# Transposes as two 64-row halves, the middle column once a batch, and a narrowing with fewer VectorE steps, in a fused Performer attention and FNet kernel

## The chip, the cores and the metric

The kernel runs on one core of one Trainium2 chip. The metric is the device time of one execution in microseconds. The times and the profile are taken on the chip. A profile comes from one execution, and its time is not exactly the median of the timed runs. The engines are called PE (TensorE products), PEld (TensorE weight loads), DVE (VectorE), ACT (ScalarE), POOL (GpSimd) and SP (SyncE, which issues the DMAs).

## The reference

Everything is float32 at the end; the inputs come as float64 and are narrowed on the chip. B = 8 batches, H = 8 heads, S = 576, D = 64, 128 random features, model width 512, hidden width 2048.

```python
# attention with positive random features
q_p, k_p = phi(q * scale), phi(k * scale)   # phi(x) = exp(h - max(h)), h = x @ omega.T - |x|^2/2
kv, z = k_p.T @ v, k_p.sum(over s)
x = (q_p @ kv) / (q_p @ z + 1e-6)           # heads side by side: (B, 576, 512)
# Fourier mix and MLP
u = x + real(fft(fft(x, axis=1), axis=2))
un = (u - mean(u)) / sqrt(var(u) + 1e-6)
out = u + relu(un @ w_ch1) @ w_ch2
```

## The kernel before

The program has two stages. The first works through attention, the Fourier mix, the loading and narrowing of the weights, four plain blocks of 128 tokens of the MLP and the sums of weights that the second stage needs. The second stage does the other 4096 tokens, in eight blocks of 512, with a Strassen-like scheme of seven products: `first_of` (L1310) makes the hidden layer, and `product_of` (L1490) the output.

The order of all instructions is written out ahead. Each piece of work is a generator that yields a `Step` (engine or engines, a planned duration, the events it needs, the buffers and PSUM banks it takes and gives) and then issues its instructions. `Listing.run` picks the next step. In the first stage the string `PICKS` says which, one character for a step: the place of the stream in the list of waiting ones, and whether a step that two engines can do goes to the second. In the second stage the planner itself picks by planned times. Every engine, and SP's DMA queue, then runs its own list in this order. An instruction that waits holds up all that is behind it on its engine.

PSUM has eight banks. `take=("bank",)` takes one and `take=("duo",)` takes two adjoining ones that begin at an even number. A bank is given back by the step that empties it.

**Attention** (`attn`, 32 head pairs, three streams of them at a time). The rows of k and q of a pair are nine and nine in a tile `kq`. `transposed` turns nine 128x128 squares of it (L512) into banks in groups of 4, 4 and 1, each group into one bank, and `evicted` copies a group to `kqT` on ACT (L528) or DVE (L526). `pairs_of` multiplies by omega (L606): the first six pairs with tiles of 64 rows and all 128 columns of the array ("wide"), the others with tiles of 64 by 64. `softmax` takes row maxima (L549, DVE) and exponentials (L566, ACT) into `e`. Products with v follow (L640, 64 by 64 tiles). Then nine squares of the queries' features are turned in groups of 1, 4 and 4 (L512 again, to `qeT`), multiplied (L687, L695, tiles of 128 by 64) and divided into x (L716 on DVE, or ten scaled copies L712 on ACT).

**Mix** (`mix`, once a batch). `folds` adds and subtracts mirrored rows and columns (L743 to L779, DVE or POOL). The transform along the tokens is L799 and L809, copied to `y` by ACT (L822). Then for each of three blocks of rows c (128, 128 and 64 rows) L849 does the transform along the width. The middle column of the fold goes a way of its own: after L849 in each block, four products of one column each (L860, two records each) put its transform into one more column of the same bank. `residual` fetches the bank with ACT (L893), the column with it, and combines and adds to x (L898 to L911).

**Narrowing** (`narrow`, 32 slabs of 128x512, two 32-bit words a number, `lo` and `hi`). The high word is scaled by ACT (L439) or POOL (L437); DVE takes the sign (L442), shifts and joins (L444), takes the exponent (L447) and scales the low word with it (L449). POOL or DVE adds the two (L455). A weight so made is what L1099 and L1122 of the plain blocks and the sums of weights wait for.

**Norms and plain blocks.** `norm_of` normalises 128 tokens; for the plain blocks and for the first large one it turns four squares on PE into one bank (L1035), which ACT copies out (L1039). `plain_of` has the products L1099 (hidden) and L1122 (output). They fill PE between attention steps.

**Sums of w2** (`w2_parts`). For each of seven factors, up to eight subtractions (L1196, POOL or DVE) make summed quarters of w2, and five stores (L1219, L1221) send them to `w2l` in memory. The next factor's subtractions wait for all five.

Of the kernel before, what the change touches and what calls it, by code (L numbers as in the profile page):

```python
# [39 lines left out]
class Clock(NamedTuple):  # L40
# [16 lines left out]
DIGITS = "0123456789abcdefghijklmnopqrstuvwxyzABCDEFGHIJKLMNOPQRSTUVWXYZ!#$%&()*+,"  # L57
# [6 lines left out]
    "40e0f03eafdaegebg3NbcbeefdcOdeccfgdb37ghj0gjj7hlP79Kj7ik97i8S7efhjffeHldfPiehdjfdOShgihidaKOdbRhciff"  # L64
    "ecgOfeejdfdPdeeedgSfdffdOfd8Kiii88jhd8jP8b99i8e8jcddghjgheiifcecdciieicgPgdef9cdghbkededfgchbggb79ij"
    "8hi7hjaPN97aj9gfffeg8eif8hcej1jccc7ehidbhffLiQObfbeG766gggfcbjahj9Ofghhjj8dgkkgT6jghff8de6dUjfhbgegh"
    "MefRafjUf8jgciSjeckkhjakkaeikggjlioklnRSgodonON7l7l6nnj9icadc97cibPJIej788a7edhclhkmjjagVijihkkfpVim"
    "oklilTTillaghlhnmVjkmpjkhhnmkimlgglmbjpjjg9d9alafhhdjlacdTback0j766k7lh4g89Gck6gkki77gij5ijhgj6dimni"
    "3ndjgi6Kc4jldlaikbkaijbhf75dcjlmUVUDGci45jciekajkkUk5kihoUeaeobaiodlenMSdonbiiljjcWjjkboijjkkhgMfkik"
    "hiflkmOFF99nol5m8jT7naabda89Rbj97ecdl8cjilegiPkQb4acahg57ebbgabgdjkdTkk6eceebb5f9dg4RGce486ggg6egfhh"  # L70
    "fg4g9egf5cbdRgfhhhcgjhggejigibbmHnbedijj6Neb7biihi9bgihckaffPa8cijdhbdghbaeibdefffacjiciQSfi9JJ75ih5"
    "jgjI699ajfg6g7fgefd65bO6Kalkkgd5jgjikagfldliPJpeoaeeOPQNejadgilgicljiSSFe65k56kl5Hk7j67S9lilk9gliih6"
    "ffUgec4fg4dbgg7fedaif5gfbheefilddddddeQhg9kbfncggRcfkkafkag6ngb65p5Hopoj4bhoaXbelli68bjjl5b7dlhiQRhi"
    "lflhpkgiWomjknmmmUimnjbjhnJjkm5akPFgedccff6Wf7idUVhi8Th3fogbqp8fgmkeidjna7ckeXYghmnmffnjeo79q6547oa4"
    "nlkpd7aceonnc8bViVicilbhmjim8fh7Snn8l5mkkPjgfRhfhihg8ghfbS4kjf83j4lllb79jei8mnUblfnmmiolpilOki9Mh5l5"
    "pmnaOm79jjVmkbblekFiji9a9kffjgjikhiihfgjafhgfigh4g50fff0ba5fdh9dghda77hgfdcbg8eO988jcehefibjjkellPcc"
    "fcdhgcihPgcffba2f82b3c98cbcdcd6a299efgddb9KGQQbefLa9ecf74gg9867RgP9idg8kgOhePP7be6ff2e5cc8fbMgdaf8f8"
    "9hd9bM999bddc7cdb7ec9effegd7ibhgeQ8hKf7ccghRlUikh7m5lWmm5dkMQ6M71fS6d1gdb99747ifddh8fdhhdhfdbihgiljn"
    "gWgijgQ93ekal8kEhIIbT3jjagkb9k9eTfhkhlje34m49974i666h68fa7e6eHK79982975a894a39M8cM8b4aK7ab984fgO8ebc"
    "J8b86ce8Pb5fc9cbe6caff3a9b94f8dIQe9abd876e9fdcFPdb7ffbf99SS8RiLa4a7gPbajfgg8gdfhg2i2787Hf6OcdIN5d3LH"  # L80
    "accd46ddeaa72d9c7bbaa4bb9a9bc7c0777dghhdP7Bfddebd76ff1fddIe9949438686bcGaca8F348dHc67a5be95Hb55d15E4"
    "9Gc1F5a9a6844634458E584E59189970955888574443113301110"
# [39 lines left out]
class Listing:  # L122
# [4 lines left out]
    def __init__(self, buffers):  # L127
        self.clock = FIRST
        self.free = dict.fromkeys((PE, ACT, DVE, POOL, SP, NONE, PORT), 0.0) | self.clock.begin
        self.buffers = {name: [0.0] * n for name, n in buffers.items()}  # L130
        self.made = {}
        self.moved = 0.0
        self.mode = "whole"
        self.banks = [0.0] * 8
        self.got = None

    def banks_at(self, n, t):
# [3 lines left out]
        for i in range(0, 8, n):  # L141
# [6 lines left out]
    def start(self, step, ready, before, other=False):  # L148
# [30 lines left out]
        engines = sorted(step.engines, key=lambda e: begin(e) + step.engines[e])  # L179
        eng = engines[other and len(engines) > 1]  # L180
# [3 lines left out]
    def run(self, streams, picks=None):  # L184
        todo = []
        picks = iter(picks or ())
        clock = self.clock
# [15 lines left out]
        while todo:  # L203
            pick = next(picks, None)
            other, n = divmod(DIGITS.index(pick), 36) if pick else (0, 0)
# [75 lines left out]
def kernel(  # L281
# [128 lines left out]

    tabs = _tables(S, DM)
# [15 lines left out]
    def narrow(i, dst, raw):  # L427
# [3 lines left out]
        lof, hif, bits = lo.bitcast(F32), hi.bitcast(F32), dst.bitcast(U32)  # L431


        step = Step({ACT: 0.57, POOL: 1.48}, after=(("raw", i),), port=True, bias=1.11)
# [3 lines left out]
        else:  # L438
# [4 lines left out]
        yield Step(DVE, 1.05, port=True, bias=0.36)  # L443
# [3 lines left out]
        nc.vector.tensor_scalar(sign[:], bits, 0xFF800000, None, op0=ALU.bitwise_and)  # L447
        yield Step(DVE, 0.61, give=("sign",), port=True, bias=-0.99)
        nc.vector.scalar_tensor_tensor(  # L449
            lof, lo, 2.0**-52, sign[:].bitcast(F32), op0=ALU.mult, op1=ALU.mult  # L450
        )
        step = Step({POOL: 1.25, DVE: 0.61}, makes=("w", i), give=("slab",), port=True, bias=1.25)
        yield step
        eng = nc.gpsimd if step.eng == POOL else nc.vector
        eng.tensor_tensor(out=dst, in0=dst, in1=lof, op=ALU.add)  # L455
# [38 lines left out]

    def transposed(src, name, groups, after, makes, give, order=None):
# [3 lines left out]
        for j0, j1 in groups:  # L499
# [3 lines left out]
                0.109 * m,  # L503
                after=after(j0, j1),
                take=("bank",) + (("turned",) if j0 == 0 else ()),
# [5 lines left out]
            for j in range(j0, j1):  # L511
                nc.tensor.transpose(ps[:, (j - j0) * 128 : (j - j0 + 1) * 128], src(j), ident[:])  # L512
            yield Fork(evicted(dst, b, j0, j1, makes, order))
        return dst

    def evicted(dst, b, j0, j1, makes, order):
# [13 lines left out]
        ps = psum_of(b)[:, 0 : 128 * (j1 - j0)].rearrange("q (c p) -> q c p", p=128)  # L530
        dst = dst[:, j0:j1, :]
        if order is None:
            copy(dst, ps)
            return
        h, s, t = order[j0]
        dst = dst.rearrange("q c p -> q (c p)").rearrange("q (h s t c) -> q s h t c", h=h, s=s, t=t)
        ps = ps.rearrange("q c (h t s) -> q s h t c", h=h, s=s)
# [35 lines left out]
    def attn(n):  # L573
# [9 lines left out]
            ((0, 4), (4, 8), (8, R)),  # L583
# [8 lines left out]
        def pairs_of(js, *ts):  # L592
# [3 lines left out]
                (0.25 if wide else 0.23) * len(js),  # L596
                mode="rows" if wide else "quarters",
                after=(("kqT", n, js[-1] // 4 * 4), "om2"),
# [24 lines left out]
        def feature(c):  # L623
# [6 lines left out]
            1.1,  # L630
# [18 lines left out]
        def keep():  # L649
# [23 lines left out]
            1.22,  # L673
# [54 lines left out]
    def mix(b):  # L728
# [5 lines left out]
        mid_t = small.tile([P, NC3, 1], F32, name="mid", tag="mid", bufs=2)  # L734

        def folds(n):
            op = (ALU.add, ALU.subtract)[n]
            even, odd = (ALU.subtract, ALU.add) if n else (ALU.add, ALU.subtract)
            step = Step({DVE: 1.135, POOL: 2.75}, take=("half",), port=True)
# [15 lines left out]
            step = Step({DVE: 0.91, POOL: 1.55}, port=True)  # L755
            yield step
            eng = nc.gpsimd if step.eng == POOL else nc.vector
            for dst, o in ((NC3, ALU.add), (1, ALU.subtract)):
# [7 lines left out]
                {DVE: 1.2, POOL: 2.2},  # L766
# [11 lines left out]
            middle = fold[:, :, 3, 0:1] if n else mid_t[:]  # L778
            eng.tensor_copy(out=middle, in_=h[:, 1 : NC3 + 1, QD : QD + 1])  # L779

        yield from folds(0)
        yield Fork(folds(1))

# [47 lines left out]
        for c in range(NC3):  # L831
# [3 lines left out]
                1.38 if c < NL else 0.94,  # L835
                mode="whole" if c < NL else "halves",
                after=tuple(("y", b, n) for n in range(2)) + ("cd", "sd"),
# [17 lines left out]
            def middle(i):  # L855

                g, odd = divmod(i, 2)
                rows = slice(64 * odd, 64 * odd + 64) if g else slice(0, 128)
                k1 = HK * odd + k0 + NK * g
                nc.tensor.matmul(  # L860
                    ab[p1 + w * odd : p1 + w * odd + w, 1, KD : KD + 1],
                    lhsT=cs[rows, k1 : k1 + w],
                    rhs=mid_t[rows, 1 if g else NL * (1 - odd), :],
                    start=g == 0,
                    stop=g == 1,
                    skip_group_check=True,
                )
# [4 lines left out]
            for i in range(4):  # L872
                middle(i)
# [758 lines left out]
```

## Time and profile before

| | us |
|---|---|
| median of three runs | 1166.79 |
| lowest and highest | 1164.52, 1167.47 |
| profiled execution: time | 1174.67 |
| profiled execution: span | 1172.2 |
| granted TensorE clock, mean | 0.996 |
| first L1310 product starts (end of the first stage) | about 424 |

| engine | busy us in the span | share |
|---|---|---|
| PE | 1153.5 | 98% |
| PEld | 1032.9 | 88% |
| DVE | 754.7 | 64% |
| ACT | 436.8 | 37% |
| POOL | 430.4 | 37% |

A busy time is the union of an engine's instructions. A PE record runs from its start until its last result is out (0.27 us for 128 columns), while the next may start 0.109 us after it, so PE's busy time does not say how full the array is; distances from start to start do. A float32 product gives two records, a transpose only one. Idle time of an engine is put down to what released the instruction after it.

### The profile page before, as it was taken

How to read it: one execution, taken by the hardware profiler on the slowest of the kernel's cores; microseconds unless marked ns; L12 is line 12 of the kernel's file. 1: busy time of each engine (PE TensorE's matmuls, PEld its weight loads, DVE VectorE, ACT ScalarE, POOL GpSimd, SP SyncE). 2: the span in 40 equal slices, each digit the busy share in tenths (PEclk: the TensorE clock that was granted, in tenths of full speed). 3: DMA queues.
4: the chain of work that ended last, by engine and by line, in shares of the span. 5: the costliest groups of instructions: out<-in, count | busy, mean ns of one | idle time of the engine just before them, and what ended most of it. 6: DMA issues, size and time to landing. Idle time of an engine off the chain costs nothing.

```text
span 1172.2 us, 31328 instructions
## 1 busy us (share of the span) xinstructions
PE 1153.5 (98%) x12437; PEld 1032.9 (88%) x12437; DVE 754.7 (64%) x1573; ACT 436.8 (37%) x1485; POOL 430.4 (37%) x496
## 2 busy tenths in 40 slices
PE   8999999999999999999999999999999999999998
PEld 7888888779777868998998998898999899899898
DVE  5999999986676655744754664573573574474255
ACT  6998898866444212122112212212212212221211
POOL 2433444455472106225225324413513512522421
PEclk8999999999999999999999999999999999999999
DMA  7866765665662254873783593694495396388055
GB/s 218 224 188 186 240 181 178 203 210 163 207 196 101 77 162 139 263 264 85 222 278 112 172 308 99 152 317 141 112 319 190 82 290 231 83 258 263 35 166 203
DMA packets 167217, 220.34 MB, mean 188 GB/s; under 512 B 50080, under 2 KB 81056, under 8 KB 167072
## 3 DMA queue, kind: packets, MB, share of 16 engines
q1 hardware_dynamic: 166576, 218.09, 60.7%
q8 instruction: 98, 1.61, 0.6%
q14 instruction: 47, 0.39, 0.1%
q10 hardware_dynamic: 496, 0.26, 0.1%
HBM read 179.24 MB, written 43.25 MB: 190 GB/s over the span
## 4 chain that ended last, share of the span: by engine, by line
PE 88%; DMA 5%; DVE 4%; ACT 2%; SPq 1%; issue 1%; DVEq 0%
PE banks L1310 33%; PE banks L1490 27%; PE banks L1099 5%; PE banks L606 5%; PE banks L1122 4%; PE banks L512 4%; DMA wl<-w2l 3%; PE banks L640 2%; PE banks L687 2%; PE banks L849 2%; PE banks L799 1%; ACT e L566 1%; DVE nmx L549 1%; DMA kq<-in_k_dram 1%; PE banks L809 1%; PE banks L860 1%
## 5 line engine op out<-in xcount | busy, mean ns | idle before, releaser
L1490 PE MATMUL banks<-wl,sums 128*128 128x128 f32 x1792 | 217.4, 275 | 0.0
L1490 PEld LDWEIGHTS banks<-wl,sums 128*128 128x128 f32 x1792 | 208.6, 192 | 0.0
L1296 DVE CUSTOM_DVE_ANT_0 hid<-banks,s 128x256 f32<-128x256 f32 x192 | 80.9, 424 | 188.8 <-PE banks L1310 188.8
L566 ACT ACTIVATE e<-banks,nmx 128x128 f32<-128x128 f32 x576 | 165.3, 434 | 23.2 <-DVE nmx L549 22.4
L1324 ACT ACTIVATE s<-banks 128x256 f32<-128x256 f32 x192 | 73.7, 384 | 259.0 <-PE banks L1310 259.0
L1310 PE MATMUL banks<-unT,w 128*128 128x256 f32 x704 | 166.3, 379 | 0.0
L1310 PEld LDWEIGHTS banks<-unT,w 128*128 128x128 f32 x704 | 133.2, 190 | 18.3 <-issue 0.5
L1530 POOL TENSOR_TENSOR ur<-ur,part 128x512 f32<-128x512 f32 x32 | 47.3, 1479 | 267.1 <-ACT part L1523 187.0
L1465 ACT ACTIVATE s<-banks 128x128 f32<-128x128 f32 x168 | 46.6, 278 | 256.7 <-PE banks L1490 220.3
L1310 PE MATMUL banks<-tt,w1s 128*128 128x256 f32 x512 | 126.3, 379 | 0.0
L1310 PEld LDWEIGHTS banks<-tt,w1s 128*128 128x128 f32 x512 | 97.0, 190 | 13.7 <-DVE hid L1296 0.4
L1490 PE MATMUL banks<-wl,hid 128*128 128x128 f32 x768 | 100.0, 276 | 3.2 <-DMA wl<-w2l 3.1
L1470 DVE TENSOR_TENSOR part<-banks,s 128x128 f32<-128x128 f32 x168 | 49.0, 292 | 83.4 <-PE banks L1490 82.2
L549 DVE TENSOR_REDUCE nmx<-banks 128x8 f32<-128x1024 f32 (+1 forms) x96 | 89.3, 951 | 19.7 <-PE banks L606 15.5
L1490 PEld LDWEIGHTS banks<-wl,hid 128*128 128x128 f32 x768 | 94.0, 192 | 6.0 <-DMA wl<-w2l 4.5
L606 PE MATMUL banks<-om,kqT 64*64 64x128 f32 (+1 forms) x2088 | 80.6, 278 | 1.9 <-ACT kv L656 1.2
L1310 PE MATMUL banks<-unT,w1s 128*128 128x256 f32 x320 | 79.5, 379 | 0.0
L606 PEld LDWEIGHTS banks<-om,kqT 64*64 64x64 f32 (+1 forms) x2088 | 65.8, 140 | 13.3 <-issue 4.3
L1490 PE MATMUL banks<-wl,hs 128*128 128x128 f32 x576 | 75.1, 275 | 0.5 <-DVE part L1470 0.4
L1490 PEld LDWEIGHTS banks<-wl,hs 128*128 128x128 f32 x576 | 70.1, 192 | 1.2 <-DVE part L1470 0.6
L1377 POOL TENSOR_TENSOR hs<-hid,hs 128x256 f32<-128x256 f32 x64 | 50.1, 784 | 57.2 <-issue 37.1
L1310 PEld LDWEIGHTS banks<-unT,w1s 128*128 128x128 f32 x320 | 60.4, 190 | 8.7
(128 smaller groups left out, 1914.6 us busy)
## 6 DMA issues: line engine op xcount, KB each, us to landing
wl<-w2l SPq DMA_DIRECT2D x392, 256.0 KB
raw<-in_moe_w_ch_dram SPq DMA_DIRECT2D x32, 512.0 KB
kq<-in_k_dram SPq DMA_DIRECT2D x32, 288.0 KB
kq<-in_q_dram SPq DMA_DIRECT2D x32, 288.0 KB
vd<-in_v_dram SPq DMA_DIRECT2D x32, 288.0 KB
u<-us SPq DMA_DIRECT2D x36, 256.0 KB
ur<-us SPq DMA_DIRECT2D x36, 256.0 KB
out_dram<-ur SPq DMA_DIRECT2D x34, 256.0 KB
```

What stands on the lines that cost most here:

```text
L512: nc.tensor.transpose(ps[:, (j - j0) * 128 : (j - j0 + 1) * 128], src(j), ident[:])
L549: nc.vector.tensor_reduce(nmx[:, :, 0:num], pps[:, :, 0 : MF * num].rearrange("p b (c m) -> p b c m", m=MF), axis=AX.X, op=ALU.max, negate ...
L566: nc.scalar.activation(out=e[:, c + (i if num == 1 else 0), :], in_=pps[:, i, MF * c : MF * c + MF], func=AF.Exp, bias=nmx[:, i, c : c + 1],)
L606: nc.tensor.matmul(pps[cols, c, MF * m : MF * m + MF], lhsT=kqT[rows, j, cols], rhs=om2[rows, :],)
L1099: nc.tensor.matmul(hp[:, 0:TP], lhsT=w1[:, dc, 128 * fc : 128 * fc + 128], rhs=unTs[key][:, dc, :], start=(dc == 0), stop=(dc == NDC - 1),)
L1296: nc.vector._custom_dve(TENSOR_ADD_SAT, out=o, in0=ps, in1=sb, s0=FMAX, s1=0.0)
L1310: nc.tensor.matmul(ps[:, 0:HT].rearrange("f (b q) -> f b q", q=Q), lhsT=left(dc), rhs=right(dc), start=start and dc == 0, stop=(dc == D2 - 1),
L1324: nc.scalar.activation(out=s[:], in_=ps[:, 0:HT], func=AF.Copy)
L1377: nc.gpsimd.tensor_tensor(out=o, in0=l, in1=r, op=op)
L1470: nc.vector.tensor_tensor(out=part[:, t, 128 * m : 128 * m + 128], in0=ps[:, 0:128], in1=saved[with_][:], op=ALU.add,)
L1490: nc.tensor.matmul(ps[:, 0:128], lhsT=left[:, f], rhs=wls[j, i, n][:, f], start=start and f == 0, stop=(f == 3), skip_group_check=True,)
L1530: eng.tensor_tensor(out=o, in0=o, in1=other, op=ALU.add)
```

## The change

- **Transposes.** `turned_by` replaces each transpose of a 128x128 square (L512, L1035) by two of 64 rows and 128 columns. The halves use rows 0 to 63 and 64 to 127 of the array and write into two adjoining banks, so a group takes a `duo`. `halves_of` is the view of the two banks that the copies read. `kqT` is turned in two groups, 4 and 5 squares, where there were three.
- **Middle column.** The four one-column products after each L849 go. A step `middles` makes those of all three blocks of a batch together, in one bank, with operands padded with zeros so that all use 128 rows, and two small ACT copies keep the result in `mid_k`.
- **Narrowing.** ACT converts the low word to an integer scaled by 2^-29, DVE's L447 and L449 go, and POOL always does the last addition, now on integers.
- **Stores of w2's sums.** One step a store in place of one for all five; the next subtractions wait for the stores of the tiles they overwrite and no others.
- **Order.** A new `PICKS`, two characters a step: stream and engine as before, and the bank. Some planned durations are changed.

```diff
 class Listing.run
-            other, n = divmod(DIGITS.index(pick), 36) if pick else (0, 0)
+            n = place(pick) if pick else 0
+            other, self.bank = divmod(place(next(picks)), 9) if pick else (None, None)
 narrow
-        lof, hif, bits = lo.bitcast(F32), hi.bitcast(F32), dst.bitcast(U32)
+        hif, bits = hi.bitcast(F32), dst.bitcast(U32)
+        def rounding():
+            yield Step(ACT, 0.57, after=(("raw", i),), makes=("low", i), bias=1.11)
+            nc.scalar.activation(out=lo, in_=lo, func=AF.Copy, scale=2.0**-29)
+        yield Fork(rounding())
...
-        nc.vector.tensor_scalar(sign[:], bits, 0xFF800000, None, op0=ALU.bitwise_and)
-        yield Step(DVE, 0.61, give=("sign",), port=True, bias=-0.99)
-        nc.vector.scalar_tensor_tensor(
-            lof, lo, 2.0**-52, sign[:].bitcast(F32), op0=ALU.mult, op1=ALU.mult
-        )
-        step = Step({POOL: 1.25, DVE: 0.61}, makes=("w", i), give=("slab",), port=True, bias=1.25)
-        yield step
-        eng = nc.gpsimd if step.eng == POOL else nc.vector
-        eng.tensor_tensor(out=dst, in0=dst, in1=lof, op=ALU.add)
+        yield Step(POOL, 1.25, after=(("low", i),), makes=("w", i), give=("slab",), port=True, bias=1.25)
+        nc.gpsimd.tensor_tensor(out=bits, in0=bits, in1=lo, op=ALU.add)
 new functions
+    def turned_by(ps, n, src):
+        y = 512 // n
+        for c in range(len(src)):
+            for a in range(2):
+                rows = slice(64 * a, 64 * a + 64)
+                out = ps[:, a].rearrange("q (h y) -> q h y", h=n)[:, :, 64 // n * c : 64 // n * (c + 1)]
+                nc.tensor.transpose(out, src[c][rows], ident[rows, rows])
+    def halves_of(ps, n, m):
+        flat = ps.rearrange("q b f -> q (b f)").rearrange("q (h y) -> q h y", h=2 * n)
+        return flat[:, :, 0 : 64 // n * m].rearrange("q h (c x) -> q h c x", c=m)
 transposed
-                0.109 * m,
+                0.03 + 0.056 * m,
+                mode="rows",
-                take=("bank",) + (("turned",) if j0 == 0 else ()),
+                take=("duo",) + (("turned",) if j0 == 0 else ()),
-            for j in range(j0, j1):
-                nc.tensor.transpose(ps[:, (j - j0) * 128 : (j - j0 + 1) * 128], src(j), ident[:])
-            yield Fork(evicted(dst, b, j0, j1, makes, order))
+            n = order[j0][0] // 2 if order else 1
+            turned_by(ps, n, [src(j) for j in range(j0, j1)])
+            yield Fork(evicted(dst, b, j0, j1, n, makes, order))
 evicted
-        ps = psum_of(b)[:, 0 : 128 * (j1 - j0)].rearrange("q (c p) -> q c p", p=128)
+        ps = halves_of(psum_of(b), n, j1 - j0)
 attn
-            ((0, 4), (4, 8), (8, R)),
+            ((0, 4), (4, R)),
 mix
-            def middle(i):
-                g, odd = divmod(i, 2)
...
-            for i in range(4):
-                middle(i)
+    def middles(b, mid_t, mid_k):
+        yield Step(PE, 0.5, mode="halves", after=(("fold", b, 0), "cs"), take=("bank",))
+        mb, ps = got()
+        for c in range(NC3):
+            w = 64 if c < NL else 32
+            for g in range(2):
+                for odd in range(2):
+                    k1 = HK * odd + 64 * c + NK * g
+                    col = 2 + odd if g else 1 - odd
+                    nc.tensor.matmul(
+                        ps[w * odd : w * odd + w, c : c + 1],
+                        lhsT=cs[:, k1 : k1 + w],
+                        rhs=mid_t[:, col : col + 1],
+                        start=g == 0, stop=g == 1, skip_group_check=True,
+                    )
+        yield Step(ACT, 0.22, give=(mb,), makes=("mid", b))
+        for c, n in ((0, P), (2, 64)):
+            nc.scalar.activation(out=mid_k[0:n, c : c + 2 - c // 2], in_=ps[0:n, c : c + 2 - c // 2], func=AF.Copy)
 norm_of
-        yield Step(PE, 0.437, take=("bank",), give=("u",))
+        yield Step(PE, 0.25, mode="rows", take=("duo",), give=("u",))
-        for dc in range(NDC):
-            nc.tensor.transpose(
-                tp[:, 128 * dc : 128 * dc + 128], u[:, 128 * dc : 128 * dc + 128], ident[:]
-            )
+        turned_by(tp, 2, [u[:, 128 * dc : 128 * dc + 128] for dc in range(NDC)])
 w2_parts
-            yield Step(SP, 3.0, 4.0, after=(("w2t", i),), kb=7 * 256, makes=("w2l", i))
             for n, t in ((0, c11), (1, c21), (4, c22)):
+                yield Step(SP, 0.6, 2.6, kb=256, makes=("w2l", i, n))
...
+            of_big = stored[0:3] if part is summed else of_big
+            of_sums = stored[3:5]
```

## The prediction

> **What bounds the kernel now.** I read the windows first, because the kernel has two stages. Up to about 424 us attention, the Fourier mix, the weight conversion and four plain blocks of the MLP share the chip. After that come the large products.
>
> ```profile
> 10.00:60.00 50.00, 47.67 (x1009) 41.10 (x1008) 44.79 (x79) 43.29 (x162) 18.10 (x12) 0.94 0.78 224
> 60.00:250.00 190.00, 187.26 (x3999) 158.64 (x3998) 178.25 (x404) 158.17 (x560) 83.72 (x86) 1.00 0.64 191
> 250.00:424.00 174.00, 171.82 (x2465) 136.39 (x2463) 114.39 (x266) 76.42 (x280) 71.22 (x73) 1.00 0.49 153
> ```
>
> Columns: stretch and length, then busy us of PE, PEld, DVE, ACT and POOL, granted clock, DMA share, GB/s. PE is busy 406.8 of 414 us. DVE comes next with 178.3 of 190 (94%) in the middle stretch, then 66%. The instruction lists of the two programs show the same PE order, instruction for instruction, from the first L1310 product on. The change therefore acts before 424 us only. The chain and PE's waits agree that PE sets this stretch:
>
> ```profile
> PE 88%; DMA 5%; DVE 4%; ACT 2%; SPq 1%; issue 1%; DVEq 0%
> PE banks L512 <- DMA kq<-in_k_dram: 2.8, 2, 2.3
> PE banks L1099 <- DVE qeT L526: 1.7, 1, 1.7
> PE banks L606 <- ACT kv L656: 1.2, 2, 0.7
> ```
>
> Waits (total us, times, longest) are small. Counting each start against the shortest start-to-start of its kind, I find 29 us lost on PE between 10 and 424 us. Hence PE time saved there should come off the end nearly one for one. Third, the groups and the order of time give the prices:
>
> ```profile
> L512 PE MATMUL banks<-ident,e 128*128 128x128 f32 x288 | 43.8, 280 | 1.8 <-DVE kqT L526 0.9 <-ACT e L566 0.9
> L512 PE MATMUL banks<-ident,kq 128*128 128x128 f32 x288 | 43.4, 287 | 2.9 <-DMA kq<-in_k_dram 2.8
> L449 DVE SCALAR_TENSOR_TENSOR raw<-raw,sign 128x512 f32<-128x512 uint32 x32 | 22.0, 687 | 0.6
> L447 DVE TENSOR_SCALAR sign<-w 128x512 uint32<-128x512 uint32 x32 | 15.2, 476 | 1.1
> L439 ACT ACTIVATE w<-raw 128x512 f32<-128x512 f32 x24 | 18.6, 788 | 3.7 <-DMA raw<-in_moe_w_ch_dram 3.7
> ```
>
> ```profile
> 30.76 1.28 PE L640 MATMUL banks<-vd,e 64*64 64x65 f32 x72
> 31.97 0.49 PE L606 MATMUL banks<-om,kqT 64*128 64x128 f32 x4
> ...
> 34.00 1.09 PE L512 MATMUL banks<-ident,e 128*128 128x128 f32 x8
> 35.02 1.16 PE L606 MATMUL banks<-om,kqT 64*128 64x128 f32 x16
> 36.11 1.09 PE L512 MATMUL banks<-ident,kq 128*128 128x128 f32 x8
> ```
>
> ```profile
> 232.83 0.60 PE L512 MATMUL banks<-ident,e 128*128 128x128 f32 x4
> ...
> 233.71 0.61 PE L849 MATMUL banks<-cd_sb,y 128*128 128x129 f32 x4
> 234.25 0.49 PE L860 MATMUL banks<-mid,cs_sb 128*64 128x1 f32 x8
> 234.67 0.71 PE L849 MATMUL banks<-sd_sb,y 128*128 128x129 f32 x4
> ...
> 236.18 0.66 PE L512 MATMUL banks<-ident,e 128*128 128x128 f32 x4
> ```
>
> Columns: start us, length, then the records; 64*128 is the part of the array used. Each run ends one pipeline latency (0.27) after its last start. So four squares in 0.60 start (0.60-0.27)/3 = 0.109 apart.
>
> **Squares as halves.** 576 squares (L512) and 32 (L1035) become 1216 half squares, whose moving side has 64 columns instead of 128. A square's 0.109 per 128 columns makes 0.055 per 64. L606's tiles of 64 rows show that two row halves run together, loads included: 16 records of 128 columns fill the 1.09 from 35.02 to 36.11, or 0.068 each, where one by one they would need 16 x 0.109 = 1.74. What could spoil it is the weight load, now as long as the product. A run behind another array shape lasts 0.66 instead of 0.60, so a square's load costs 0.06 where it is not hidden. Bounds for a pair of halves: 0.055 (load hidden) and 0.055 + 0.06 = 0.115 (not hidden: no gain). I take 0.057, because L640 is the nearest row: 18 records in each of four tiles, 65 columns and a load of their own every time, fill 31.97 - 30.76 = 1.21 less a shape change of 0.15, so 0.059. Gain: 608 x (0.109 - 0.057) = **31.6 us**; at the bounds 32.8 and -3.6.
> [...]
>
> **Shape changes.** A half square uses 64*128, so a run beside whole-array products now changes shape and one beside wide L606 no longer does. In the lists, leaving out the middle column, changes go from 193 to 236. Price: the last of eight squares starts at 34.00 + 0.06 + 7 x 0.109 = 34.82 and L606 at 35.02, 0.20 later instead of 0.109, so 0.09, and 0.06 for the exposed load: 0.15. 43 x 0.15 = **-6.5 us**.
> [...]
>
> **Middle column.** The last L849 before L860 starts at 233.71 + 3 x 0.112 = 234.05. Without L860 the next would start at 234.16; it starts at 234.67 and shows a load of 0.10 besides (0.71 against 0.61): 0.61 each time. The 64-row block costs 0.37 in the same way. Per batch 2 x 0.61 + 0.37 = 1.59, over eight 12.7 us. Now it is one run per batch of 24 records. Eight records in two shapes took 0.42, so 0.3 for the records and two or three changes of 0.15, 0.7 in all: 5.6. Gain **7.1 us** (6 to 8). Its result is fetched by two small ACT copies well before L849 asks for it.
>
> **Narrowing and the other engines.** L447, L449 and four L455 leave DVE: 15.2 + 22.0 + 2.8 = 40.0. The new assignment gives back 20 more subtractions of w2 (13.7), 34 more qeT copies (20 x 0.21 + 14 x 0.42 = 10.1) and about 10 in small pieces. DVE goes from 337 to some 331 us. ACT gains 32 conversions; no integer one is shown, and L439 (same shape and stride, 0.775 by busy time) gives 24.8. Bounds: 0.60, an L528 copy of 512 columns by busy time (29.3/49), and twice L439; I take L439. Against that it loses 30 scaled copies of x, 34 qeT copies, 25 kqT copies (a group of five in place of four and one), 13 hidden blocks and four L439, about 30 us together. POOL does all 32 final additions (4 x 1.35), now on integers: between 1.35 and 2.7 each, and I take 1.35, the row of the same shape. It loses 20 subtractions of w2 (26). So ACT stays near 276 and POOL near 160 of some 385 us, both under cover of PE; at the upper bounds ACT reaches 300 and POOL 205, still under it. If POOL's addition is late, weights arrive late, and the next to wait is L1099 behind them in PE's queue. Splitting the wait before the w2l stores lets SP issue earlier and is worth nothing on the path: SP has no share beyond 1%. The extra wait of L849 for the middle column holds up what stands behind it on PE, but its products are at least five PE runs earlier in the list.
>
> **The sum.** 31.6 - 6.5 + 7.1 = 32.2 us of PE time. PE's 29 us of loss are 7% of the stretch; with less PE work between the same DVE and ACT steps I let them grow by 3. Gain 29. The profiled execution has a span of 1172.2 and a time of 1174.7, 7.9 above the median of 1166.8. Its span would become 1143 and its time 1145.7; the median 1166.8 - 29 = **1138 us**.
>
> **Rivals.**
> *Banks (slower).* Every run of squares now takes two adjoining banks out of eight, where it took one, beside the pairs that L606, L640, L687, the mix and a bank held through L1122 need. There are 5 x 32 + 8 = 168 such runs. A mean wait of 32/168 = 0.19 us per run eats the gain; at 0.25 us the time is 1167 + 10 = 1177. For it: POOL, ACT and DVE empty these banks, and DVE stands at 94%. Against it: waits of PE for a release by ACT or DVE add up to a few us now, and a run holds its banks for half the PE time. [...]
> *Loads of the two halves do not overlap their products or each other.* Each square then costs 2 x 0.057 = 0.114: -3 - 6.5 + 7.1 makes -2.4, so 1169, no change. Against it stand L606's rows at 0.068.
> *DVE holds PE back.* If from 60 to 250 us, where DVE is 94% busy, each of the 96 reductions L549 releases PE 0.15 us later than now, 14 us go: 1152. For it, DVE sheds only 6 us in total while PE sheds 32.
> *More comes.* The first 60 us have DVE 97% busy around 20 to 50 us; the lists show 26.5 to 22.6 us of DVE work for the first four pairs, and PE's loss there could shrink. With 10 us of it gone: 1128.
>
> **How the numbers follow.** What a measurement can tell from no change is about 0.3%, 3.5 us. Forecast (1130 to 1146) 0.62, DVE 0.17, more 0.08, overlap missing 0.03, banks 0.10. Faster 0.62 + 0.17 + 0.08 = 0.87, same 0.03, slower 0.10. The range takes the first three cases, 1126 to 1158.
>
> **What would show it.** Right: stage two starts near 395 us with an unchanged length; nine squares of a pair start about 0.057 apart per square; about 250 shape changes of 0.09; L860's successor is one run of about 0.5 per batch; DVE near 86% before that point. Wrong: pairs of halves start 0.1 apart; PE's waits for ACT or DVE at the squares rise above 30 us (banks); POOL's addition well over 1.35 and L1099 waiting for it; PE busy the same but stage two no earlier.

## The result and the profile after

The kernel after takes 1184.55 us (median of four runs, 1182.08 to 1186.27) against 1167.13 us: a ratio of 1.015 [1.0125, 1.0176], 17 us slower where 29 us faster was predicted. Its profiled execution took 1184.30 us with a span of 1182.5. Stage two starts at 431.8 us and lasts 750.7, against 423.8 and 748.4 (a second profile of the kernel before gave 419.5 and 749.0). So nearly all of the loss lies before stage two. One of the four executions of g_pair_halves, an experiment below, took 1955.1 us at a mean granted clock of 0.555 and is left out of every figure. Here are the same stretches of the kernel after, and the chain of waits over the whole span:

```profile
10.00:60.00 50.00, 44.58 (x1122) 38.36 (x1120) 45.31 (x94) 45.24 (x154) 20.27 (x16) 1.00 0.72 209
60.00:250.00 190.00, 170.81 (x3685) 141.21 (x3686) 161.28 (x338) 133.93 (x438) 84.77 (x82) 0.98 0.66 203
250.00:424.00 174.00, 169.75 (x3230) 134.23 (x3229) 140.25 (x327) 98.12 (x348) 47.89 (x56) 1.00 0.45 138
```

```profile
PE 83%; DVE 7%; DMA 4%; ACT 3%; issue 2%; SPq 0%; POOL 0%; DVEq 0%; ACTq 0%; POOLq 0%
```

In the middle stretch PE falls from 187.3 to 170.8 busy us, but DVE falls as well (178.3 to 161.3) and so does ACT (158.2 to 133.9). No engine is as full as PE and DVE were (99% and 94%). The new work itself runs near its prices:

```profile
L525 PE MATMUL banks<-ident,kq 64*128 64x64 f32 x576 | 28.4, 232 | 7.0 <-DVE ht L1127 1.6 <-DMA kq<-in_q_dram 1.2 <-DVE x L754 1.0
L478 POOL TENSOR_TENSOR w<-w,raw 128x512 uint32<-128x512 uint32 x32 | 42.8, 1340 | 68.8 <-DVE w L474 29.7 <-DVE rden L742 10.8 <-ACT raw L461 8.4
L461 ACT ACTIVATE raw<-raw 128x512 uint32<-128x512 uint32 x32 | 22.7, 715 | 0.3 <-DMA raw<-in_moe_w_ch_dram 0.3
```

The order of time of PE shows both the price and what eats it:

```profile
107.86 0.77 PE L525 MATMUL banks<-ident,kq 64*128 64x64 f32 x18 [1.58 <-DVE ht L1127]
108.56 1.28 PE L678 MATMUL banks<-vd,e 64*64 64x65 f32 x72
...
132.81 1.70 PE L678 MATMUL banks<-vd,e 64*64 64x65 f32 x95
138.34 0.97 PE L678 MATMUL banks<-vd,e 64*64 64x65 f32 x49 [3.82 <-issue]
```

Nine squares as 18 halves take 0.77: the last half starts 0.55 after the first and lasts 0.22. The second pair of halves starts 0.11 after the first, and each later pair 0.062 or 0.063 after the one ahead. The prediction took 0.057. But the run came 1.58 us late, and further on PE stood for 3.82 us, waiting for nothing that the profile shows. PE's longest waits before stage two (total us, times, longest):

```profile
PE banks L678 <- issue: 4.4, 3, 3.8
PE banks L644 <- DVE kqT L564: 2.8, 3, 1.6
PE banks L644 <- ACT e L604: 2.2, 5, 0.6
PE banks L678 <- DVE bmp L951: 1.8, 3, 1.2
PE banks L525 <- DVE ht L1127: 1.6, 1, 1.6
```

### The profile page after: what moved, and what is told of

Its sections match the earlier page's. It is cut to its first block, busy times and chain, and to the rows that moved or that the text cites. A ratio compares the mean times of both kernels' runs of the same rounds, so it can differ in the third digit from the quotient of the medians.

```text
span 1182.5 us, 32511 instructions
## 1 busy us (share of the span) xinstructions
PE 1140.8 (96%) x13045; PEld 1016.3 (86%) x13045; DVE 767.1 (65%) x1591; ACT 435.1 (37%) x1423; POOL 412.4 (35%) x483
## 4 chain that ended last, share of the span: by engine, by line
PE 83%; DVE 7%; DMA 4%; ACT 3%; issue 2%; SPq 0%; POOL 0%; DVEq 0%; ACTq 0%; POOLq 0%
PE banks L1359 33%; PE banks L1539 28%; PE banks L1166 4%; PE banks L644 4%; PE banks L1143 4%; PE banks L525 3%; DMA wl<-w2l 3%; PE banks L678 2%; ACT e L604 2%; PE banks L725 2%; DVE nmx L587 1%; PE banks L894 1%; PE banks L844 1%; DMA kq<-in_q_dram 1%; DVE w L474 1%
## 5 line engine op out<-in xcount | busy, mean ns | idle before, releaser
L604 ACT ACTIVATE e<-banks,nmx 128x128 f32<-128x128 f32 x576 | 157.8, 406 | 41.8 <-DVE nmx L587 41.5
L1519 DVE TENSOR_TENSOR part<-banks,s 128x128 f32<-128x128 f32 x168 | 48.9, 291 | 86.5 <-PE banks L1539 85.4
L644 PEld LDWEIGHTS banks<-om,kqT 64*64 64x64 f32 (+1 forms) x2088 | 67.1, 141 | 23.3 <-ACT e L604 4.1
L1426 POOL TENSOR_TENSOR hs<-hid,hs 128x256 f32<-128x256 f32 x64 | 50.0, 782 | 57.6 <-issue 37.5
```

The costliest lines, as they stand in the source:

```text
L604: nc.scalar.activation(out=e[:, c + (i if num == 1 else 0), :], in_=pps[:, i, MF * c : MF * c + MF], func=AF.Exp, bias=nmx[:, i, c : c + 1],)
L644: nc.tensor.matmul(pps[cols, c, MF * m : MF * m + MF], lhsT=kqT[rows, j, cols], rhs=om2[rows, :],)
L1426: nc.gpsimd.tensor_tensor(out=o, in0=l, in1=r, op=op)
L1519: nc.vector.tensor_tensor(out=part[:, t, 128 * m : 128 * m + 128], in0=ps[:, 0:128], in1=saved[with_][:], op=ALU.add,)
```

## The ledger

For every kernel I split the time from 10 us to the start of stage two as the prediction did. **Loss** is the time on PE beyond the shortest start-to-start of each kind of neighbours; **work** is the rest. "Half clock" is the time before stage two in which the granted clock was at half. Ratios are against the kernel before on the same chip, with their 95% interval. All times but that of the second profile of before are medians of timed runs; the other columns come from one profile each. How the shortest distances are taken moves work and loss of a kernel by some 3 to 8 us, so small differences between rows say nothing. Only a part of the loss stands in the profile as waits of over 0.15 us: 27 us of it in after, 6 in the second profile of before.

| kernel | us | ratio | stage two at | work | loss | half clock |
|---|---|---|---|---|---|---|
| before, second profile | 1170.3 | one run | 419.5 | 383.8 | 25.7 | 0 |
| after | 1184.6 | 1.015 [1.0125, 1.0176] | 431.8 | 358.5 | 63.3 | 6.8 |
| a_whole | 1186.5 | 1.0178 [1.0151, 1.0204] | 440.7 | 381.8 | 48.9 | 6.8 |
| a_oldnarrow | 1221.3 | 1.046 [1.0428, 1.0492] | 467.1 | 367.3 | 89.8 | 41.0 |
| a_old | 1222.0 | 1.0489 [1.0463, 1.0516] | 473.7 | 393.4 | 70.3 | 23.9 |
| b_narrow | 1184.0 | 1.0155 [1.0132, 1.0178] | 434.7 | 385.4 | 39.3 | 10.2 |
| b_mid | 1175.5 | 1.0055 [1.0037, 1.0073] | 427.7 | 387.7 | 30.0 | 3.4 |
| b_mid_dve | 1172.3 | 1.0014 [0.9997, 1.0031] | 422.9 | 386.6 | 26.3 | 0 |
| b_dve | 1168.0 | 0.9993 [0.9979, 1.0006] | 418.2 | 384.0 | 24.2 | 0 |
| b_light | 1159.1 | 0.9916 [0.9901, 0.9931] | 410.5 | 359.0 | 41.5 | 3.4 |
| a_shift | 1184.8 | 1.0133 [1.0108, 1.0157] | 429.1 | 359.3 | 59.8 | 10.2 |
| a_shift_whole | 1184.0 | 1.012 [1.0095, 1.0145] | 434.8 | 382.4 | 42.4 | 3.4 |
| b_greedy | 1218.5 | 1.0404 [1.0382, 1.0425] | 473.4 | 388.3 | 75.1 | 27.3 |
| g_halves | 1235.9 | 1.056 [1.0539, 1.0581] | 484.1 | 367.2 | 106.9 | 34.1 |
| g_whole | 1201.7 | 1.0267 [1.0249, 1.0285] | 453.4 | 383.7 | 59.7 | 10.2 |
| a_greedy | 1221.9 | 1.0439 [1.0416, 1.0461] | 462.5 | 360.9 | 91.6 | 37.5 |
| g_pair_whole | 1221.6 | 1.0441 [1.0407, 1.0475] | 475.6 | 387.1 | 78.5 | 17.1 |
| g_pair_halves | 1234.2 | 1.0546 [1.0503, 1.059] | 482.1 | 369.1 | 103.0 | 41.0 |
| g_pair_light | 1222.6 | 1.0457 [1.0431, 1.0482] | 468.8 | 365.5 | 93.3 | 37.5 |

The kernel after does 25 us less work on PE (383.8 to 358.5) and loses 38 us more (25.7 to 63.3). The halved clock can explain little of it: at half clock the squares of before start 0.214 us apart in place of 0.109, and the L1143 products of after 0.214 in place of 0.112, so 6.8 us there cost at most 3.4. The question is where the rest comes from.

## Experiments: parts undone in the new order

**Whole squares.** The order, narrowing and middle column of after; squares whole again, in the banks that the order gives them.

```diff
-                nc.tensor.transpose(out, src[c][rows], ident[rows, rows])
+            nc.tensor.transpose(flat[:, 128 * c : 128 * c + 128], src[c], ident[:])
```

> The changed kernel with whole squares instead of halves, in its own order: a group of four lies in one bank, five in two. TensorE has 608 x 0.052 = 32 us more to do and about 43 shape changes of 0.15 less, net 25. Theory A (order): part of it falls into TensorE's waits, 10 to 25 us slower than the changed kernel, 1195 to 1210. Theory B (bank pairs): the waits of 34 us go with the pairs, so 1170 to 1185, no slower than the changed kernel. Theory C says nothing else than A here.

PE has 23 us more work (358.5 to 381.8) and the kernel is 2 us slower, in neither range. The halves' gain is real on PE and turns into loss almost whole, in two places. By the profiles stage two starts 8.9 us earlier with halves (431.8 against 440.7), so some 14 us are lost before it. And it lasts 4.6 us longer (750.7 against 746.1): PE waits there 7.0 us for loads of `wl`, in a_whole 1.6. In the six profiles with halves these waits are 4.1 to 7.2 us, in the fourteen others 0 to 3.4. Why was not tested.

**Old narrowing.** After, with the four DVE operations of before and the addition in floats.

```diff
-            nc.scalar.activation(out=lo, in_=lo, func=AF.Copy, scale=2.0**-29)
+        nc.vector.tensor_scalar(sign[:], bits, 0xFF800000, None, op0=ALU.bitwise_and)
+        nc.vector.scalar_tensor_tensor(lof, lo, 2.0**-52, sign[:].bitcast(F32), op0=ALU.mult, op1=ALU.mult)
```

> The changed kernel with the old narrowing at the same places in the order: L461 on ACT goes, DVE gets back the two operations on the low word, POOL's addition is a float32 one again. Theory A and B: DVE has 37 us more to do between 10 and 250 us where it is 85% busy, so 5 to 20 us slower than the changed kernel, 1190 to 1205. Theory C (the conversions on ACT delay the exponentials and so TensorE): 10 to 20 us faster, 1165 to 1175.

37 us slower than after, more than either theory had: in this order the new narrowing is worth more than all else.

**Old work in the new order.** Whole squares, old narrowing, middle column after each block. The groups of `kqT` (4 and 5), the stores and the choice of engines stay those of after.

> The changed kernel's order of steps with all of the old work in it: whole squares (a group of four in one bank), the old narrowing (the low word's two DVE operations back, nothing on ACT), four middle products after each L894. Theory A (the new order itself loses the time, the parts gain some 25 us): 1184 + 25 to 45, so 1205 to 1230 against 1167 before. Theory B (pairs of banks make TensorE wait): with single banks the waits go and the old work comes back, so about 1165 to 1180. Theory C (the narrowing's load on ACT and POOL makes the waits): as B, 1165 to 1180, and the run with the old narrowing alone must show it too.

1222.0 us, as Theory A has it: the old work in the new order is 55 us slower than the kernel before. With the old narrowing in place, halves and middle column together bring 0.7 us. So the new order does not suit the old work.

## Experiments: parts alone in the old order

The halves could not be put into the old order: at some of its groups no pair of adjoining banks is free. The other parts could.

**New narrowing.** ACT's rounding, integer addition, two DVE operations less; all steps where they were.

> The kernel before with the new narrowing alone, each instruction at the old step's place: ACT's conversion of the low word beside the high word's, no L447 and L449, POOL or DVE adding integers as the old order has it. Theory A and B: DVE is freed of 37 us where it was 94% busy, TensorE stays the bound, so 1150 to 1167. Theory C: ACT, 83% busy from 60 to 250 us, gets 25 us more and holds the exponentials up: 1172 to 1185.

17 us slower, as slow as after. The 25 us of conversions show on ACT, now 171.5 of 190 us (90%) in the middle stretch, where DVE fell to 150.6:

```profile
60.00:250.00 190.00, 183.62 (x3950) 155.96 (x3950) 150.55 (x345) 171.45 (x594) 80.54 (x81) 1.00 0.64 193
```

**DVE's time alone.** The same, but the rounding is one DVE operation in the place of two.

```diff
-        nc.vector.tensor_scalar(sign[:], bits, 0xFF800000, None, op0=ALU.bitwise_and)
-        nc.vector.scalar_tensor_tensor(lof, lo, 2.0**-52, sign[:].bitcast(F32), op0=ALU.mult, op1=ALU.mult)
+        nc.vector.tensor_scalar(lo, lo, 2.0**-29, None, op0=ALU.mult)
```

> The kernel before in its old order; the narrowing adds integers as the kernel after does, the low word rounded on DVE in one operation in the place of two (476 and 687 ns), nothing added to ACT: some 18 us of DVE less before stage two, TensorE untouched. Theory A, in the old order DVE is late often enough to be worth a part of its time, as TensorE was (10 us of 30): 1160 to 1164 us, faster than both kernels. Theory B, DVE is covered in the old order: 1166 to 1169 us. Theory C, any moved end of a step upsets the old order: 1170 us or more.

No change (0.9993 [0.9979, 1.0006]). So it is the conversion's move to ACT that made b_narrow slow, and DVE's time alone (25 us less in the profile) is worth nothing in the old order. It was not only the time that ACT spends on it. The two profiles have the same records on PE in the same order; b_narrow falls 16.4 us behind b_dve, and 11.5 of this before 60 us. Some 7 us come from one place in b_narrow:

```profile
36.49 0.65 ACT L436 ACTIVATE raw<-raw 128x512 uint32<-128x512 uint32 x1 [5.76 <-DMA raw<-in_moe_w_ch_dram]
```

```profile
38.22 1.97 PE L509 MATMUL banks<-ident,e 128*128 128x128 f32 x8 [5.38 <-ACT e L563]
```

A conversion stood in ACT's list ahead of its weights' arrival, the exponentials behind it waited, then PE, and the granted clock was at half from 34.6 to 41.4 us.

**Middle column once a batch.** All its products at the first block; the way it was written, not all of its sums are added up, so it prices time only.

```diff
-            for i in range(4):
-                middle(i)
+            if c == 0:
+                for i in ((0, 1), (2,), (3,)):
+                    for cc in range(NC3):
+                        for ii in i: middle(ii, cc)
```

> The kernel before, its old order and everything else, but the middle column's twenty-four records of a batch are run together at the first of the three chunks (the 128-row products of all chunks, then the 64-row ones), and ACT copies three columns out once (16 more copies of some 0.2 us, 3 us in all). TensorE saves the changes of shape at two of three chunks, by the prediction's prices some 5 to 6 us in eight batches. Theory A, in the old order TensorE is the pace before stage two (88% of the chain of waits), so this comes off: 1161 to 1163 us. Theory B, it is eaten by waits as in the new order: 1166 to 1168 us.

> As the kernel that runs the middle column once a batch, in the old order; besides, the narrowing adds integers as the kernel after does, but the low word is rounded on DVE in the place of the two old DVE operations (476 and 687 ns), so ACT gets nothing more and DVE saves some 0.55 us for each of 32 slabs, 18 us before stage two. Theory A, what made the new narrowing lose 17 us in the old order was ACT's 25 us alone: without them this is no slower than the kernel with the middle column alone and up to 6 us faster, 1155 to 1163 us. Theory B, the old order loses with any other narrowing, since its waits were fitted to the old one: 1170 us or more.

The test missed its aim. By starts, the one-column records took 11.4 us in place of 9.5, and PE's work rose from 383.8 to 387.7. They still change between 128 and 64 rows; that this is the reason is my estimate. It came out 0.55% slower. With the low word rounded in one DVE operation besides, it is 3 us faster than b_mid and can't be told from the kernel before.

**The same TensorE saving without the rest.** The squares are turned by one product of the upper 16 bits, in the old order, in one bank.

```diff
-                nc.tensor.transpose(ps[:, (j - j0) * 128 : (j - j0 + 1) * 128], src(j), ident[:])
+                nc.tensor.matmul(ps[:, (j - j0) * 128 : (j - j0 + 1) * 128], lhsT=src(j).bitcast(BF16)[:, 1::2], rhs=ident[:].bitcast(BF16)[:, 1::2])
```

> The kernel before in its old order, every step where it was; only each square is turned by a product of the upper 16-bit halves of its words with the identity's (the lower 16 bits are left out), in one bank as before. One such product streams 128 columns once and should take near 0.055 us where the square took 0.109, so TensorE saves up to 608 x 0.054 = 33 us, about what the prediction gave the halves, without pairs of banks, without changes of shape and without a new order. Theory A, in the old order TensorE is the pace and its time comes off one for one, as the prediction read the old profile: 1134 to 1142 us, stage two from 391 to 399. Theory B, the old order's copies and loads are nearly as late as TensorE, so most of the saving turns into waits: 1152 to 1164 us. Theory C, it is eaten whole: 1165 us or more.

A square takes 0.060 us (a run of four starts at 101.63 us, the run behind it at 101.87); the expected 0.055 was an estimate that no earlier run had shown. PE's work is that of after within what the ledger can tell (359.0 and 358.5). The kernel gains 10 us, not 25, as Theory B has it: the loss grew from 25.7 to 41.5. The middle stretch and PE's longest waits in this kernel:

```profile
60.00:250.00 190.00, 180.29 (x4150) 148.02 (x4152) 179.20 (x402) 160.13 (x572) 91.25 (x91) 1.00 0.67 201
```

```profile
PE banks L1040 <- DVE u L1033: 2.2, 1, 2.2
PE banks L517 <- ACT e L571: 2.1, 6, 0.5
PE banks L517 <- DMA kq<-in_q_dram: 2.0, 1, 2.0
```

DVE stands at 94% of the stretch and ACT at 84%. Once PE is shorter, they and the loads are next, in small pieces: over the pieces of the chain before stage two, PE's share is 59%, DVE's 21% and ACT's 11%. This kernel beats both others, but only by leaving out the lower 16 bits of what it turns, so it is no replacement for them.

## Experiments: is DVE the pace of the new order?

The sign is left out of the narrowing in after, with halves and with whole squares.

```diff
-        nc.vector.tensor_scalar(sign[:], hi, 0x80000000, None, op0=ALU.bitwise_and)
-        nc.vector.scalar_tensor_tensor(bits, bits, 3, sign[:], op0=ALU.logical_shift_left, op1=ALU.bitwise_or)
+        nc.vector.tensor_scalar(bits, bits, 3, None, op0=ALU.logical_shift_left)
```

> The kernel after, order and all, but the narrowing leaves the sign out: the mask (456 ns) is gone and the shift with the OR (813 ns) is a shift alone, one operation of some 0.45 us for each of 32 slabs, so DVE has 26 us less before stage two and nothing else changes. Theory A, the new order is paced by DVE (putting the old narrowing back, 38 us more on DVE and 23 less on ACT, cost 37): 10 to 26 us faster than after, 1158 to 1174 us. Theory B, it is paced by many short waits of fixed length and by no engine: under 6 us, 1179 us or more.

> As the kernel after without the sign in the narrowing, and with whole squares in the place of the halves, in the same order. With all of the narrowing the halves were worth 2 us (1184.5 against 1186.5). Theory A, DVE hid the gain of the halves: with DVE lighter, whole squares are slower than halves by 8 us or more. Theory B, DVE did not hide it: the two are within 5 us of each other again.

DVE's busy time went from 767.1 to 742.3 us. With halves next to nothing came off (a ratio of 1.0133 where after has 1.015), so Theory A of a_shift fell. With whole squares some 7 us did (1.012 where a_whole has 1.0178; stage two starts 6.0 us earlier). So DVE is not the pace of the new order with halves, and a small part of it with whole squares. Between the two, halves are again worth nothing (1184.8 and 1184.0 us on one chip): DVE did not hide their gain. With PE (a_whole) and DVE each worth little there, waits between engines are what is left; this is an inference, as ACT and the loads were not tried alone.

## Experiments: halves and banks in the planner's own order

To have an order fitted to each variant I gave no picks, so that the planner chooses step by step by its own planned times, as in stage two.

> The kernel before with the order that its own planner picks step by step, instead of the written-out one. It is the base of the three runs beside it. An order that nobody searched is slower than the written-out one: 1190 to 1220 against 1167.

> The kernel before with the halves alone (three groups of kq as before, each in two banks), order picked by the planner for this work. Theory A (the parts are worth their price wherever the order is made for them): 15 to 30 us faster than the planner-ordered kernel before. Theory B (bank pairs): no faster than it, within 8 us, or slower. Theory D (in this stage TensorE is no longer what sets the pace once an order has waits in it): 0 to 10 us faster.

> The planner's own order with the new narrowing, the new middle column and the new stores of w2's sums, but whole squares in single banks. Theory A: 5 to 15 us faster than the planner-ordered kernel before (middle column 7, DVE 40 us less). Theory C (ACT's conversions cost): slower than it by 5 to 20. Theory D: DVE sets the pace of such orders, so 15 to 35 us faster.

> All of the changed kernel's work in the order that its planner picks step by step. Theory A: 25 to 45 us faster than the planner-ordered kernel before, and perhaps below the changed kernel's 1184. Theory B: the gain of the run with whole squares is lost again, within 10 us of the planner-ordered kernel before. Theory D: as fast as the run with whole squares, within 8 us, since TensorE's time is not the pace.

Halves cost 17 us on the old work (1218.5 to 1235.9) and 20 on the new (1201.7 to 1221.9), each in an order of its own. Narrowing, middle column and stores gain 17 and 14. PE's waits of over 0.15 us for ACT's copies of `kqT` and `qeT`, which give the banks back, rose from 2.5 to 21.6 us on the old work, so the banks rival seemed the cause. Three kernels with exactly the same steps in the same order on every engine tested it: pairs of banks held with whole squares, with halves, and with the 16-bit products of b_light.

> The kernel before in the order that its planner makes step by step, old narrowing, old middle column, whole squares; but each group of squares holds a pair of banks until its copy (four squares use one bank of it, five use both). Beside it stand the same with single banks (1218.5 us) and with halves in pairs of banks (1235.9). Theory A, the pair of banks is what costs: TensorE has the old work and the pairs too, so this is slower than both, near 1235.9 + 26 = 1262 us (1245 to 1275), and TensorE's waits for ACT's copies of kqT and qeT stay near 28 us. Theory B, the pairs cost nothing and the halves lose for another reason (their copies, their changes of shape): 1218 us, give or take 8, with such waits under 6 us.

> The same steps in exactly the same order on every engine as the kernel with whole squares in pairs of banks; only the squares are turned as halves. So the difference of the two is TensorE's saved time (some 26 us by the prediction's terms) and nothing else of the order. Theory A, saved TensorE time comes off where TensorE is late and is eaten by waits elsewhere: faster than its twin by 5 to 18 us. Theory B, it comes off one for one as the prediction had it: faster by 24 to 28 us. Theory C, all of it is eaten, as in the order of the kernel after (2 us of 26): within 4 us of its twin.

> The order made by the planner with a pair of banks for each group, as in the twins with whole squares (1221.6 us, 17 us at half the granted clock) and with halves (1235.8 us, 41 us at half clock); the squares are turned by products of the upper 16-bit halves of their words (the lower 16 bits are left out), as short for TensorE as the halves, but with all 128 rows. Theory A, the clock falls to half after a stretch of 3.4 us in which TensorE's work, weighed by the share of rows and columns that it uses and by its columns, is under 0.36 of what fits: the shorter squares leave as little such work as the halves, so it loses like them, 1228 to 1240 us with 30 us or more at half clock. Theory B, something in the halves themselves costs (64 rows, two banks written): without it TensorE's saved time comes off, 1195 to 1212 us.

Holding pairs costs 3 us (1218.5 to 1221.6), within what another order can do, though the same waits rise to 13.5 us. So in the planner's order the pair is not what costs. Yet the halves lose 13 us in one and the same order, with 18 us less PE work, where every theory had them faster or level. By the profiles half of it lies before stage two (6.6 us) and half in it (6.4). The stretch from 20 to 160 us, whole squares first, then halves, then light:

```profile
20.00:160.00 140.00, 118.42 (x2456) 102.86 (x2455) 124.34 (x250) 103.27 (x357) 37.93 (x29) 0.96 0.58 172
```

```profile
20.00:160.00 140.00, 115.64 (x2566) 100.80 (x2569) 121.72 (x249) 100.35 (x350) 35.75 (x28) 0.89 0.57 170
```

```profile
20.00:160.00 140.00, 112.97 (x2490) 98.67 (x2482) 125.43 (x252) 103.05 (x359) 38.46 (x29) 0.91 0.58 175
```

The granted clock (third number from the end) falls from 0.96 to 0.89 and 0.91. Both shortened kernels spend 41.0 and 37.5 us at half clock instead of 17.1, which is up to 12 and 10 us of PE time lost. The light squares neither gain nor lose (1222.6): neither theory's figure. Theory A's border is an estimate; the last section counts the windows. What makes the halves some 12 us slower than the light squares stays open. They have 308 changes of shape where the other two have 244, and more loss in waits below 150 ns, but at half clock starts lie about twice as far apart (0.214 us in place of 0.112, L1143 of after), which the ledger counts as loss too, and I cannot part the two.

**The kernel before again.**

> The kernel before once more, unchanged, for a second profile. Theory A, the first profile was late in its first stage by its slow start (the clock at half for 6.8 us from 9.2 us on): stage two starts near 416 to 420 us and lasts 748 as before. Theory B, the 7.5 us lie in stage two: stage two starts near 424 and lasts some 742.

Theory A holds: stage two starts 4.3 us earlier, with no time at half clock (6.8 us in the first profile), and lasts the same (749.0 and 748.4).

## Why the prediction was wrong, point by point

- **Halves, 31.6, and shape changes, -6.5: near in sum.** 25.1 predicted, 23.3 measured (work of a_whole less that of after). The price of a square was too low: 0.062 to 0.063, not 0.057, which makes 28 us. Against it, after has only 28 shape changes more than a_whole, where 43 were priced.
- **Middle column, 7.1: too high.** L860's 9.5 us by starts became 6.3, and all work besides the squares fell by 2 us (383.8 to 381.8). In sum PE's work fell by 25.3, where 32.2 was predicted.
- **POOL's integer addition, 1.35 each: right** (1.340), and POOL held nobody up for long. ACT's conversion took 0.71 where 0.775 was taken. DVE was priced at 331 us before stage two and had 350.
- **"PE time saved there should come off the end nearly one for one": wrong even in the old order.** There 25 us of PE work gave 10 (b_light). The 88% of the chain that the prediction put beside it are of the whole span, and stage two, 748 of 1172 us, is 94% PE. The same chain between 10 and 424 us:

```profile
by line: PE banks L1099 13.8%; PE banks L606 13.0%; PE banks L1122 12.3%; PE banks L512 12.3%; PE banks L640 6.6%; PE banks L687 5.5%; PE banks L849 4.6%; PE banks L799 3.7%; ACT e L566 3.5%; DVE nmx L549 3.2%; PE banks L809 2.3%; PE banks 
```

The view ends the line there. All pieces of that chain sum to PE 78%, DVE 10% and ACT 6%, and before 60 us to DVE 35% and PE 31%. In after PE has 61%. A share says who is the latest now, not by how much: DVE at 94% and ACT at 83% of the middle stretch stood close behind.
- **"I let them grow by 3": this is the step that failed.** The loss grew by 37.6. Some 16 of it came in the old order too, with as little PE work (b_light). The other 22 lie between b_light and after, which have the same PE work, and 25 us in time. These two differ in the order, in the halves themselves and in the work moved between engines; the runs don't part the 22 us among them. The prediction took the order as free. It counted waits that the trace of before showed and let the new order inherit them, though every step had another place.
- **Narrowing "under cover of PE": wrong on both sides.** It costs 17 us in one order, a good part of it at one conversion that waits for its weights, and gains 37 in the other.
- **The rivals.** Banks had the right sign and the wrong mechanism: PE's idle time ahead of the squares was 9.4 us in all in after, far below 30, and pairs cost 3 us alone in the planner's order. DVE holding PE back fell with a_shift. That loads don't overlap, which made a square 0.114, fell with the 0.062.

What stays open, besides the 22 us, is whether an order exists in which the new work beats the old kernel. None of those tried here did, and the planner's own lost 37 us more than the order of after.

## What to carry to other kernels

Read the chain of waits for the stretch that you change, not for the whole span. A share of it says who is last, not what is gained when he is quicker; look at the second and third engine of the same stretch, and expect the part of the saving that their distance allows. Where an order is written out for one set of durations, a change of work and a change of order are two changes: price the order by itself, and try the new work in the old order and the old work in the new one first. An operation moved to another engine's list brings its waits with it, not only its time. A cheap stand-in for the new operation, in the old place, shows what its saving is worth before anything is rebuilt.

## What the runs showed of the hardware

In the twenty profiles the granted clock was 1 or 0.5 at any time, and it changed on a grid of 3.41 us: it was at half for 6.83 us from 9.23 us on in before, and for 3.41 us at 139.67 and again at 194.28 in after. I weighed PE's records in each of the 6867 windows of this grid: columns times 0.85 ns (a square's 0.109 us for 128; 0.43 for the 16-bit ones, an estimate), times the share of the array's rows and columns in use. 92 windows were followed by one at half clock. Of these 89 lie under 0.37 of the window, and only 4 other windows do. By PE's busy share the best border leaves 42 wrong, and the clock fell after a window at 0.80 busy too (g_pair_halves, at 133 us). The border is fitted to these same windows, and another way of sharing out records at the edges of windows leaves 19 wrong in place of 7. So it describes these twenty profiles; it is read from their records and was not tried by itself, and why weighed records part the windows better than busy time was not shown.

PE also stood for up to 3.8 us, waiting for nothing that the profile shows (the "issue" row above); such waits of over 0.15 us were 6.0 us before stage two in after, and 0.6 in before. In the 10 us around the longest one the two queues of instructions moved three packets. Whether they have to do with the wait was not tested.
